# An adaLN block on one core: whole-tile attention, tighter KV products, LayerNorm arithmetic on GpSimd, and DMA transposes of the attention output

## The chip, the cores and the metric

The kernel runs on one core of a Trainium2 chip. The metric is device time in microseconds of one execution, the lower the better. The time of the kernel before is the median of three runs. One execution of each kernel is also recorded by the hardware profiler; all rows in this document come from such records.

## The reference, cut to what matters

One transformer block with adaptive layer norm, on 2048 tokens of 512 features (bf16), 32 heads of 16 features, and a feed-forward width of 1376.

```python
mod = silu(c) @ w_mod                      # six vectors of 512: sa, ca, ga, sb, cb, gb
h = layernorm(x) * (1 + ca) + sa
q, k, v = split_heads(h @ wqkv)            # 32 heads of 16
pq, pk = q @ w_phi, k @ w_phi              # per head
phi_q = concat(softmax(pq), softmax(-pq))  # feature map, 32 values per head
phi_k = concat(softmax(pk), softmax(-pk))
kv, z = phi_k.T @ v, sum_over_tokens(phi_k)
o = (phi_q @ kv) / (phi_q @ z + 1e-6)      # linear attention: no token-by-token matrix
x = x + ga * (o @ wo)
h = layernorm(x) * (1 + cb) + sb
x = x + gb * ((silu(h @ w_gate) * (h @ w_up)) @ w_down)
```

## The kernel before

Tokens are cut into 16 tiles of 128 and 4 chunks of 512. The program does not issue its work in source order. Every piece of work is registered with `pl.op` (line 89) with the engines that may do it, a booked duration `us`, and the buffers that it reads and writes. `Plan.run` (149) then lays all of them out on a time line of its own, with due times from `set_due` (114: each step back along a chain costs STRETCH times the booked duration plus WAIT; the matmuls marked `spine` are SPINE apart; second-norm transposes are PACE apart), and with PSUM and SBUF slots (`slots`, 227) and shares of the PSUM banks by kind (`quota`, 230). What comes out is a fixed order for each engine. On the chip an engine that meets an instruction whose input is not there waits, and all that stands behind it waits too.

Stage one runs over the 16 tiles. `first_norm` (487) makes LayerNorm statistics: `bn_stats` and `bn_aggr` on VectorE (`stats`, 340), then variance plus epsilon on VectorE, power -0.5 on GpSimd and minus mean times that on VectorE (`rstd_of`, 347), then the normalised tile `xn` on VectorE or ScalarE (`normalize`, 368). `first_T` (503) turns it feature-major on TensorE and modulates it (`modulate_T`, 380). `k_tile` (521) makes k through the folded weight `Wk2`, two exponentials on ScalarE (538, 539), their sums `S` and reciprocals `R` on VectorE (548, 549), the product `phik` on GpSimd (551), and v. `kv_tile` (554) adds phik times v into PSUM with 8 matmuls of 129 columns. `q_front` (570) makes q by chunk, and its exponentials `eT`. `gate` (588) makes ga and gb as rows; lines 625 to 631 then scale the weights `wo_sb` (4 instructions) and `wd_sb` (11) by them on GpSimd, in the middle of stage one.

After the last `kv_tile`, lines 635 to 649 write the masked sums into `KVZ`. Then `prepare(k)` (828) does two tiles at a time. `attend` (665) works on half a tile: 4 matmuls of 144 columns into the one buffer `two_ps` (2 PSUM banks), copies `Ssw`, four small VectorE instructions (690 to 695), and two that write `o2` (707). The next half can start only when `two_ps` is free again. `turn` (716) makes `oT`, feature-major: for tiles 0 and 1 by eight matmuls against the identity (726); for tiles 2 to 15 a GpSimd addition `o` (736), four TensorE transposes into a PSUM bank (735) and a ScalarE copy (739). `project` (741) multiplies by `wo`, adds to x and does the second LayerNorm; `second_T` (757) transposes and modulates again.

The feed-forward part runs over six units of two or four tiles (UNITS, 32): `ffn_gu` (773) makes gate and up by blocks of 128 of the 1376 features, `ffn_down` (807) the down projection, the sum with x (824) and the store from SP's queue (826). PSUM has 8 banks: 2 are `two_ps`, 6 are handed out one by one, of which one is an accumulator until the turn from stage one.

## Time and profile before

| | us |
|---|---|
| median of 3 runs (lowest to highest) | 248.45 (248.22 to 249.34) |
| the profiled execution: its own time | 248.46 |
| its span, first to last instruction | 246.7 |
| TensorE matmul busy in the span | 215.0 (87%) |
| VectorE busy | 174.6 (71%) |
| ScalarE busy | 128.3 (52%) |
| GpSimd busy | 101.1 (41%) |

The profiled execution is 0.01 us from the median, and 1.76 us of it lie outside the span. Busy shares over the whole span mix stages with different limits, so the table alone says only that TensorE is the busiest; the rows by stage say which engine is full where.

### The profile page before, as it was taken

To read this page: it belongs to the slowest core of one execution; us is meant where nothing else is said; L and a number is where in the kernel's file an instruction comes from. 1 tells how busy PE (TensorE), PEld (TensorE's weight loads), DVE (VectorE), ACT (ScalarE), POOL (GpSimd) and SP (SyncE) were. 2 spreads that over 40 slices of the span, in tenths; PEclk is the share of its full clock that TensorE was granted. 3 is DMA by queue.
4 is the path that set the end of the run, shared out by engine and by line. 5 is a ranking of instruction groups with operands and counts; after the bars stand their busy time and mean duration, and the time that the engine had idled before them with its cause. 6 is when DMAs were issued, how large, how long until landed. Compare 5 with 4: busy or idle time off the path is not lost.

```text
span 246.7 us, 4221 instructions
## 1 busy us (share of the span) xinstructions
PE 215.0 (87%) x1533; PEld 131.7 (53%) x1556; DVE 174.6 (71%) x461; ACT 128.3 (52%) x280; POOL 101.1 (41%) x100
## 2 busy tenths in 40 slices
PE   0799897939985879999999996999699999699994
PEld 0754555426543437777867853884345454344441
DVE  3779999996957886677767798888744798522122
ACT  2579987564763655943534524563355442355500
POOL 1117788997794011441431443353225242013300
PEclk9999999976997999999999999999999999999999
DMA  7999930000000000001001000001000001100011
GB/s 227 383 406 387 381 103 0 3 0 0 0 4 0 0 1 3 0 0 45 1 3 43 0 4 0 0 24 43 24 0 1 1 0 45 43 0 3 0 41 44
DMA packets 9062, 13.95 MB, mean 57 GB/s; under 512 B 1009, under 2 KB 6482, under 8 KB 9042
## 3 DMA queue, kind: packets, MB, share of 16 engines
q1 hardware_dynamic: 8512, 13.67, 15.4%
q8 instruction: 12, 0.20, 0.3%
q10 hardware_dynamic: 530, 0.02, 0.1%
q14 instruction: 8, 0.07, 0.1%
HBM read 11.58 MB, written 2.10 MB: 55 GB/s over the span
## 4 chain that ended last, share of the span: by engine, by line
PE 64%; DVE 24%; ACT 3%; DMA 3%; issue 3%; POOL 1%; SPq 0%; DVEq 0%; ACTq 0%
PE one_ps L786 31%; PE one_ps L818 14%; DVE S L548 5%; PE one_ps L748 5%; PE two_ps L675 3%; DVE st L343 3%; DMA wmod_sb<-in_w_mod_dram 3%; DVE xn L372 3%; PE one_ps L528 2%; PE one_ps L575 2%; DVE R L549 2%; PE one_ps L532 2%; DVE o L707 2%; ACT hT L396 2%; DVE ln_nmr L361 1%
## 5 line engine op out<-in xcount | busy, mean ns | idle before, releaser
L786 PE MATMUL one_ps<-hT,wg_sb 128*128 128x256 bf16 (+3 forms) x264 | 46.2, 308 | 1.2 <-ACT hT L396 0.9
L786 PE MATMUL one_ps<-hT,wu_sb 128*128 128x256 bf16 (+3 forms) x260 | 45.2, 307 | 0.2
L793 ACT ACTIVATE sg<-one_ps 128x512 bf16<-128x512 f32 (+2 forms) x46 | 26.3, 577 | 28.3 <-PE one_ps L786 25.2
L802 POOL TENSOR_TENSOR gu<-usb,sg 128x512 bf16<-128x512 bf16 (+1 forms) x22 | 23.5, 1070 | 42.7 <-ACT usb L800 39.9
L818 PE MATMUL one_ps<-wd_sb,gu 128*128 128x512 bf16 (+1 forms) x171 | 40.5, 379 | 0.2
L551 POOL TENSOR_TENSOR phik<-e,R 128x1024 bf16<-128x1024 bf16 x16 | 30.7, 1931 | 13.0 <-ACT hT L396 5.5
L786 PEld LDWEIGHTS <-wg_sb 128*128 128x128 bf16 (+1 forms) x264 | 25.9, 100 | 13.9 <-issue 2.1
L786 PEld LDWEIGHTS <-wu_sb 128*128 128x128 bf16 (+1 forms) x264 | 26.0, 100 | 12.2
L736 POOL TENSOR_TENSOR o<-o 128x512 bf16<-128x512 bf16 x14 | 16.1, 1152 | 38.0 <-DVE o L707 33.6
L796 DVE TENSOR_TENSOR gu<-one_ps,sg 128x512 bf16<-128x512 f32 (+1 forms) x24 | 16.3, 685 | 20.3 <-PE one_ps L786 18.4
L357 POOL TENSOR_TENSOR ln_rstd<-ln_veps,mhalf 128x1 f32<-128x1 f32 (+2 forms) x21 | 13.4, 639 | 38.3 <-DVE ln_veps L353 33.7
L818 PEld LDWEIGHTS <-gu 128*128 128x128 bf16 (+1 forms) x176 | 16.7, 98 | 17.0
L707 DVE TENSOR_TENSOR o<-two_ps,A 128x256 bf16<-128x256 f32 x64 | 24.0, 416 | 0.8
L343 DVE BATCH_NORM_STATS2 st<-x_c 128x6 f32<-128x512 bf16 x32 | 21.7, 679 | 2.7 <-DMA x_c<-in_A_x_dram 2.4
L581 ACT ACTIVATE eT<-one_ps 128x512 bf16<-128x512 f32 x32 | 17.5, 599 | 10.3 <-PE one_ps L575 10.3
L675 PE MATMUL two_ps<-KVZ,eT 128*128 128x144 bf16 x128 | 13.7, 232 | 7.3 <-DVE o L707 6.9
L548 DVE TENSOR_REDUCE S<-e 128x64 f32<-128x1024 bf16 x16 | 19.1, 1191 | 1.3 <-ACT e L539 1.2
L388 PE MATMUL one_ps<-ident_b,xn 128*128 128x128 bf16 x128 | 11.9, 236 | 7.1 <-DVE va L544 3.9
L528 PE MATMUL one_ps<-Wk,hT 128*128 128x512 bf16 x61 | 17.2, 399 | 1.0 <-ACT hT L396 0.6
L532 PE MATMUL one_ps<-wqkv_sb,hT 128*128 128x512 bf16 x62 | 17.1, 391 | 0.3 <-DVE st L343 0.2
L675 PEld LDWEIGHTS <-eT 128*128 128x128 bf16 x128 | 10.0, 100 | 13.6 <-DVE o L707 6.0
L748 PE MATMUL one_ps<-wo_sb,oT 128*128 128x512 bf16 x58 | 15.6, 380 | 1.7 <-ACT oT L739 1.4
(89 smaller groups left out, 324.6 us busy)
## 6 DMA issues: line engine op xcount, KB each, us to landing
x_c<-in_A_x_dram SPq DMA_DIRECT2D x4, 512.0 KB, 9.1
wmod_sb<-in_w_mod_dram SPq DMA_DIRECT2D x1, 2048.0 KB, 13.9
out_dram<-ot SPq DMA_DIRECT2D x16, 128.0 KB, 1.8
wqkv_sb<-in_A_wqkv_dram SPq DMA_DIRECT2D x3, 512.0 KB, 8.6
wg_sb<-in_B_w_gate_dram SPq DMA_DIRECT2D x1, 1376.0 KB, 17.5
...
```

The lines of the kernel that those rows point to most:

```text
L343: nc.vector.bn_stats(st6[:], src)
L528: nc.tensor.matmul(pk()[:], lhsT=hT[c_i][k][:, cols], rhs=Wk2[:, k, :], start=(k == 0), stop=(k == KD - 1))
L532: nc.tensor.matmul(v()[:], lhsT=hT[c_i][k][:, cols], rhs=wqkv_sb[:, k, 2 * D:3 * D], start=(k == 0), stop=(k == KD - 1))
L548: pl.op("DVE", r=[e], w=[Ss], us=1.18, fn=lambda: nc.vector.tensor_reduce(Ss()[:], e()[:], axis=AX.X, op=ALU.add))
L551: pl.op("POOL", r=[e, R], w=[bphik[i]], us=1.9, fn=lambda: nc.gpsimd.tensor_tensor(bphik[i]()[:], e()[:], R()[:].unsqueeze(3).to_broadcast ...
L675: nc.tensor.matmul(nd()[:, jj, sg * NDW:(sg + 1) * NDW], lhsT=eTs[c_i, sg, j][:, ts_], rhs=KVZ[:, sg * KD + j, :], start=True, stop=True)
L707: nc.vector.tensor_tensor(o2()[:, sg, half * HK:(half + 1) * HK, :].rearrange("p j (h d) -> p j h d", d=DH), ndv()[:, :, sg, 0:P].rearrang ...
L748: nc.tensor.matmul(a()[:], lhsT=oT()[:, j, :], rhs=wo_sb[:, j, :], start=(j == 0), stop=(j == KD - 1))
L786: nc.tensor.matmul(ps_()[0:fsz, q * n:(q + 1) * n], lhsT=wt[:, k, m * P:m * P + fsz], rhs=h2[k], start=(k == 0), stop=(k == KD - 1))
L793: pl.op("ACT", r=[g, bsilu], w=[sg], us=0.2 + 0.3 * L / CW, fn=lambda: nc.scalar.activation(sg()[0:fsz, 0:L], g()[0:fsz, 0:L], ACT.Silu))
L802: pl.op("POOL", r=[usb, sg], w=[gu], us=0.1 + 1.05 * L / CW, fn=lambda: nc.gpsimd.tensor_tensor(gu()[0:fsz, 0:L], usb()[0:fsz, 0:L], sg()[ ...
L818: nc.tensor.matmul(fp()[:], lhsT=b()[0:fsz, c0:c0 + P], rhs=wd_sb[0:fsz, m, :], start=(m == 0), stop=(m == FM - 1))
```

## The change

- `first_norm` keeps only `bn_stats` on VectorE. Ten small GpSimd instructions a group combine the six statistics into `rstd` and `nmr`. The second LayerNorm keeps `bn_aggr` on VectorE; its other arithmetic is four GpSimd instructions. `normalize` on VectorE multiplies by rstd and adds nmr.
- phi_k is laid out in 8 groups of 4 heads with both signs in one group of 128 columns. `kv_tile` still has 8 matmuls, of 65 columns instead of 129, into two banks instead of three. `KVZ` is written by four pairs of 64 partitions; all of it is zeroed at the start.
- The scaling of `wo_sb` is registered behind the last phik, that of `wd_sb` behind the first part of KVZ.
- `attend` works on a whole tile: 8 matmuls into four banks (`four_ps`, one buffer), and half as many VectorE instructions of twice the width. Those four banks are the two of the kv sums and two of the single ones, so 4 single banks are left after the turn, where there were 6; before the turn there are 6, where there were 5.
- Tiles 2 to 15 are turned by a DMA transpose from SP's queue, SBUF to SBUF, 128 KB each, booked at 2.6 us on a resource of its own (`XBAR`). The four TensorE transposes, their PSUM bank and the ScalarE copy go. There are 3 `oT` buffers instead of 2.
- Chunk 1 is one feed-forward unit of 4 tiles, not two of 2. Due times, quotas and the choice between two engines (the earliest end, not the earliest start) are new.

```diff
-UNITS = [(0, 0, 2), (0, 2, 2), (1, 0, 2), (1, 2, 2), (2, 0, 4), (3, 0, 4)]
+UNITS = [(0, 0, 2), (0, 2, 2), (1, 0, 4), (2, 0, 4), (3, 0, 4)]
-STRETCH = 1.6
-WAIT = 0.8
-SPINE = 1.2
-PACE = 11.0
+STRETCH = 2.54
+WAIT = 1.43
+SPINE = 1.1
+PACE = 8.1
+QUOTA = {'q': 2, 'turn': 4, 'T': 2, 'T2': 4, 'wo': 4, 'down': 4, 'gu': 3, 'kv': 4, 'fold': 2}
+EARLY = ("kv", "q", "fold", "T")
...
-    quota = {"q": 1, "turn": 1, "T": 2, "wo": 1, "down": 2, "gu": 4, "kv": 4, "fold": 3}
+    quota = QUOTA
...
-        pl.op("DVE", r=bmv, w=[b0], us=0.1, fn=f1)
-        pl.op("POOL", r=[b0], w=[b], us=0.4 + 0.15 * n, fn=f2)
-        pl.op("DVE", r=[b] + list(bmv), w=[bn], us=0.1, fn=f3)
+            nc.gpsimd.tensor_scalar_add(veps[:], mv_t()[:, :, 1], LN_EPS)
+            nc.gpsimd.tensor_tensor(st["rstd"][:], veps[:], mhalf[:, 0:n], op=ALU.pow)
+            nc.gpsimd.tensor_scalar(veps[:], mv_t()[:, :, 0], -1.0, None, op0=ALU.mult)
+            nc.gpsimd.tensor_tensor(st["nmr"][:], veps[:], st["rstd"][:], op=ALU.mult)
+        pl.op("POOL", r=bmv, w=[bn], us=0.8 + 0.15 * n, fn=f)
...
+        def f():
+            v = [tmp[:, i, :] for i in range(5)]
+            tt = nc.gpsimd.tensor_tensor
+            tt(v[0], st6[:, :, 1], st6[:, :, 4], op=ALU.subtract)
+            tt(v[1], st6[:, :, 2], st6[:, :, 5], op=ALU.add)
+            tt(v[2], v[0], v[0], op=ALU.mult)
+            nc.gpsimd.tensor_scalar(v[2], v[2], D / 4.0, D * LN_EPS, op0=ALU.mult, op1=ALU.add)
+            tt(v[3], v[2], v[1], op=ALU.add)
+            nc.gpsimd.tensor_scalar(v[3], v[3], 1.0 / D, None, op0=ALU.mult)
+            tt(rstd[:], v[3], mhalf[:, 0:w], op=ALU.pow)
+            tt(v[4], st6[:, :, 1], st6[:, :, 4], op=ALU.add)
+            tt(v[4], v[4], mhalf[:, 0:w], op=ALU.mult)
+            tt(nmr[:], v[4], rstd[:], op=ALU.mult)
+        pl.op("POOL", r=bst, w=[bn], us=1.6 + 0.15 * w, fn=f)
...
-                nc.tensor.matmul(kv_acc(g // 3)[:, (g % 3) * (P + 1):(g % 3 + 1) * (P + 1)],
-                                 lhsT=bphik[i]()[:, sg, 8 * j:8 * j + 8, :].rearrange("p h f -> p (h f)"),
-                                 rhs=bva[i]()[:, j, :], start=(i == 0 and g % 3 == 0), stop=(i == NT - 1),
+                nc.tensor.matmul(kv_acc(g // 4)[:, (g % 4) * (HG + 1):(g % 4 + 1) * (HG + 1)],
+                                 lhsT=bphik[i]()[:, g].rearrange("p s h f -> p (s h f)"),
+                                 rhs=bva[i]()[:, g, :], start=(i == 0 and g % 4 == 0), stop=(i == NT - 1),
...
+    for k in range(KD):
+        pl.op("POOL", r=[bgab[0], bphik[NT - 1]], w=[bwo[k]], us=1.16, fn=lambda k=k: nc.gpsimd.tensor_tensor(
+            wo_sb[:, k, :], wo_sb[:, k, :], gab[:, 0, :], op=ALU.mult))
...
+    for sg in range(2):
+        for r in range(2):
+            def fz(sg=sg, r=r):
...
+            pl.op("DVE", r=[bkv], w=[bKVZ[2 * sg + r]], us=0.65, fn=fz)
+
+    for m in range(FM):
+        fsz = fm_size(m)
+        pl.op("POOL", r=[bgab[1]] + bKVZ[0:1], w=[bwd[m]], us=1.16, fn=lambda m=m, fsz=fsz: nc.gpsimd.tensor_tensor(
+            wd_sb[0:fsz, m, :], wd_sb[0:fsz, m, :], gab[0:fsz, 1, :], op=ALU.mult))
...
-    def attend(n, half):
+    def attend(n):
...
-            for jj, j in enumerate(js):
+            for j in range(KD):
                 for sg in range(2):
...
-            tp = bank("turn", [P, KD, P], BF16)
-            o = sb("qf", "o", [P, KD, P], BF16)
-
-            def f():
-                for j in range(KD):
-                    nc.tensor.transpose(tp()[:, j, :], o()[:, j, :], ident_b[:])
-            pl.op("POOL", r=[o2, second], w=[o], us=1.15, fn=lambda: nc.gpsimd.tensor_tensor(
-                o()[:], o2()[:, 0], o2()[:, 1], op=ALU.add))
-            pl.op("PE", r=[o], w=[tp], us=0.23, fn=f)
+            o = sb("qf", "o", [P, D], BF16)
+            pl.op("POOL", r=[o2], w=[o], us=1.15, fn=lambda: nc.gpsimd.tensor_tensor(
+                o()[:], o2()[:, 0].rearrange("p j m -> p (j m)"), o2()[:, 1].rearrange("p j m -> p (j m)"), op=ALU.add))
+            pl.op("XBAR", r=[o], w=[oT], us=2.6, fn=lambda: nc.sync.dma_start(oT()[:], o()[:], transpose=True))
+            return
```

## Rows read from the trace of the kernel before

**Rows 1.** Busy by stage: window, length, busy of each engine (instructions), granted clock, DMA.

```profile
17.00:58.40 41.40, 34.24 (x293) 21.37 (x296) 40.50 (x63) 32.43 (x61) 33.37 (x23) 0.93 0.40 145
58.40:72.00 13.60, 12.93 (x91) 7.02 (x92) 8.60 (x11) 8.78 (x16) 12.08 (x8) 0.95 0.00 1
72.00:92.20 20.20, 14.75 (x94) 7.66 (x93) 16.33 (x61) 10.62 (x24) 6.11 (x7) 0.92 0.00 1
92.20:243.30 151.10, 143.51 (x974) 88.72 (x987) 98.17 (x289) 68.46 (x167) 46.89 (x50) 1.00 0.04 14
```

**Rows 2.** VectorE groups from 17 to 58.4, one shape a row: busy, mean ns.

```profile
L372 DVE TENSOR_SCALAR xn<-x_c,ln_mv,ln_rstd 128x512 bf16<-128x512 bf16 x6 | 6.6, 1140 | 0.0
L361 DVE SCALAR_TENSOR_TENSOR ln_nmr<-ln_mv,ln_rstd 128x4 f32<-128x4 f32 x3 | 3.4, 1134 | 0.0
L353 DVE TENSOR_SCALAR ln_veps<-ln_mv 128x4 f32<-128x4 f32 x3 | 1.7, 567 | 0.1
L344 DVE BATCH_NORM_AGGREGATE ln_mv<-st 128x2 f32<-128x6 f32 x9 | 1.6, 182 | 0.3
```

**Rows 3.** Timeline near the end of stage one: start, length, instruction, idle before it.

```profile
50.34 3.56 DVE L372 TENSOR_SCALAR xn<-x_c,ln_mv,ln_rstd 128x512 bf16<-128x512 bf16 x2
54.55 1.86 PE L388 MATMUL one_ps<-ident_b,xn 128*128 128x128 bf16 x16 [3.92 <-DVE va L544]
```

**Rows 4.** Costliest groups of the whole span, GpSimd, one shape a row.

```profile
L551 POOL TENSOR_TENSOR phik<-e,R 128x1024 bf16<-128x1024 bf16 x16 | 30.7, 1931 | 13.0 <-ACT hT L396 5.5 <-DVE R L549 3.9 <-PE one_ps L558 2.4
L630 POOL TENSOR_TENSOR wd_sb<-wd_sb,gab 128x512 bf16<-128x512 bf16 x10 | 11.4, 1168 | 0.0
L357 POOL TENSOR_TENSOR ln_rstd<-ln_veps,mhalf 128x4 f32<-128x4 f32 x3 | 3.0, 1006 | 0.1
L326 POOL CAST KVZ<-bm 128x64 bf16<-128x64 f32 x1 | 0.3, 290 | 0.3 <-DVE bm L316 0.3
```

**Rows 5.** The chain that ended last: start, length, engine and line, instructions.

```profile
9.32 1.02 PE one_ps L434 x32
61.56 0.35 PE two_ps L558 x6
111.58 0.45 PE one_ps L388 x8
189.81 0.86 PE one_ps L786 x4
```

**Rows 6.** Timeline of the turn from stage one to the feed-forward part.

```profile
71.38 5.63 POOL L630 TENSOR_TENSOR wd_sb<-wd_sb,gab 128x512 bf16<-128x512 bf16 x5
73.16 0.41 DVE L642 TENSOR_TENSOR KVZ<-one_ps,bm 128x256 bf16<-128x256 f32 x1
73.29 0.41 PE L675 MATMUL two_ps<-KVZ,eT 128*128 128x144 bf16 x4 [0.31 <-DVE KVZ L645]
75.13 0.81 DVE L695 TENSOR_TENSOR A<-Ssw,rden 128x32 f32<-128x32 f32 x1
76.78 0.64 PE L675 MATMUL two_ps<-KVZ,eT 128*128 128x144 bf16 x4 [2.22 <-DVE o L707]
78.47 0.19 DVE L695 TENSOR_TENSOR A<-Ssw,rden 128x32 f32<-128x32 f32 x1
78.69 0.75 DVE L707 TENSOR_TENSOR o<-two_ps,A 128x256 bf16<-128x256 f32 x2
84.26 0.75 DVE L707 TENSOR_TENSOR o<-two_ps,A 128x256 bf16<-128x256 f32 x2
92.19 1.34 PE L786 MATMUL one_ps<-hT,wg_sb 128*128 128x256 bf16 x8
```

**Rows 7.** TensorE's waits from 92.2 to 243.3: total, times, longest.

```profile
PE two_ps L675 <- DVE o L707: 2.8, 2, 1.7
```

**Rows 8.** DMA issues of the span: count, KB each, median us from issue to landing.

```profile
x_c<-in_A_x_dram SPq DMA_DIRECT2D x4, 512.0 KB, 9.1
out_dram<-ot SPq DMA_DIRECT2D x16, 128.0 KB, 1.8
```

More of the change, by code (lines that the diff above doesn't have):

```diff
@@ L133, in room @@
         for i in range(self.slots[b.tag]):
+            if b.tag == "one" and not (b.kind == f"last{i - 4}" if str(b.kind)[:4] == "last" else i < 4 or b.kind in EARLY):
+                continue
             old = live[b.tag].get(i)
@@ L225 @@
     ps = ctx.enter_context(tc.tile_pool(name="ps", bufs=1, space=PSUM))
-    slots = {"one": 6, "two": 1, "xn": 8, "nmr": 4, "ln2": 6, "WT": 2, "e": 3, "S": 3, "R": 3, "phik": 4,
-             "va": 4, "Ssw": 2, "A": 2, "o2": 3, "o": 2, "oT": 2, "sg": 3, "gu": 13,
+    slots = {"one": 6, "four": 1, "xn": 8, "nmr": 4, "ln2": 6, "WT": 2, "e": 3, "S": 3, "SS": 3, "Q": 3, "R": 3, "phik": 4,
+             "va": 4, "Ssw": 2, "A": 2, "o2": 3, "o": 2, "oT": 3, "sg": 3, "gu": 13,
              "usb": 2, "ot": 3}
-    quota = {"q": 1, "turn": 1, "T": 2, "wo": 1, "down": 2, "gu": 4, "kv": 4, "fold": 3}
+    quota = QUOTA
     pl = Plan(slots, quota)
@@ L241, in sb @@
         return Buf(tag, make)
-    two_ps = ps.tile([P, 2, CW], FP32, name="two_ps")
-    one_ps = [ps.tile([P, CW], FP32, name=f"one_ps{i}") for i in range(slots["one"])]
+    early_cm = tc.tile_pool(name="early", bufs=1, space=PSUM)
+    early = early_cm.__enter__()
+    kv_ps = early.tile([P, 2, CW], FP32, name="kv_ps")
+    one_ps = [ps.tile([P, CW], FP32, name=f"one_ps{i}")[:] for i in range(4)]
+    one_ps += [early.tile([P, CW], FP32, name=f"one_ps{i}")[:] for i in range(4, 6)]
+    blast = [Buf("one", kind=f"last{i}", keep=True) for i in range(2)]
+    four_ps = {}
     def bank(kind, shape=(P, CW), dtype=FP32):
         def make(slot):
-            ap = one_ps[slot][:] if dtype == FP32 else one_ps[slot][:].bitcast(dtype)
+            ap = one_ps[slot] if dtype == FP32 else one_ps[slot].bitcast(dtype)
             n = 1
@@ L256, in bank @@
         return Buf("one", make, kind=kind)
-    def pair():
-        return Buf("two", lambda slot: two_ps)
     pools["lnp"] = lnp
@@ L656, in f_turn @@
         modp_cm.__exit__(None, None, None)
+        early_cm.__exit__(None, None, None)
+        four_ps[0] = ctx.enter_context(tc.tile_pool(name="late", bufs=1, space=PSUM)).tile([P, KD, CW], FP32, name="four_ps")
         pools["qf"] = ctx.enter_context(tc.tile_pool(name="qf", bufs=1))
-    pl.op("NONE", r=bKVZ + bgab + [bmodB, bmodA] + bWq2, w=[bturn], us=0.0, fn=f_turn)
+    pl.op("NONE", r=bKVZ + bgab + [bmodB, bmodA] + bWq2, w=[bturn] + blast, us=0.0, fn=f_turn)
     bh2 = [[Buf() for _ in range(KD)] for _ in range(NT // 2)]
@@ L716, in turn @@
+        pl.op("DVE", r=[nd, A], w=[o2], us=1.25, fn=fo)
     def turn(n, on_pe):
-        o2, second = bo2.pop(n)
+        o2 = bo2.pop(n)
         oT = boT[n] = sb("qf", "oT", [P, KD, P], BF16)
@@ L828, in prepare @@
     def prepare(k):
-        a, b = 2 * k, 2 * k + 1
-        attend(a, 0)
-        attend(a, 1)
-        attend(b, 0)
-        turn(a, k == 0)
-        attend(b, 1)
-        project(a)
-        turn(b, k == 0)
-        project(b)
+        for n in (2 * k, 2 * k + 1):
+            attend(n)
+        for n in (2 * k, 2 * k + 1):
+            turn(n, k == 0)
+            project(n)
         h2_guard(k)
```

185 lines of the change are left out of this document (91 added, 94 removed).

## The prediction, made before the changed kernel was run

> **What bounds the kernel now.** I read the busy times by stage first, then VectorE's and GpSimd's groups inside stage one, then the chain of waits and the timeline of the turn, last TensorE's own waits in the feed-forward part. The stages have different limits [rows 1]. From 17.0 to 58.4 VectorE is busy 40.5 of 41.4 us: it is the limit, with TensorE at 34.2. From 58.4 to 72.0 TensorE is (12.9 of 13.6): the last four tiles of k, v and kv. From 72.0 to 92.2 no engine is full (TensorE 14.8, VectorE 16.3 of 20.2): this is latency, the chain attend, turn, project, norm, transpose of tiles 0 and 1, before the first gate matmul at 92.19 [rows 6]. From 92.2 to 243.3 TensorE is busy 143.5 of 151.1, the limit again; 7.6 us are idle, where a unit begins and the preparation of its tiles is late; the largest named wait is for VectorE's o, 2.8 us [rows 7]. Then 3.4 us of last addition and store, which the change doesn't touch.
>
> The sum is made against the profiled execution: span 246.7 us, 1.76 us around it, together 248.46, next to the median of 248.45.
>
> **Part by part.**
>
> *First LayerNorm, VectorE to GpSimd.* Off VectorE between 17 and 58.4 go three nmr (3.4 us), three variance-plus-epsilon (1.7) and nine aggregations (1.6) [rows 2]. An aggregation partly overlaps its neighbours, so I count 0.1 each: 3.4 + 1.7 + 0.9 = 6.0 us. VectorE idles 0.9 us there, so nearly all of it is on the path: -6.0. The nmr instructions are long (1.13 us on 4 elements) because they stand against GpSimd work, and the xn that follow may inherit that wait; so the gain could be as small as 3.
>
> GpSimd gets three groups of ten instructions in that stretch. The power takes 1.0 us; the other nine are bounded above by the 0.29 us of a 64-element cast, so at most 3.6 us a group, 2.6 us more than now [rows 4]. That is paid for by what leaves: 10 + 4 + 1 weight scalings of about 1.17 us, 17.5 us in all, of which 5 (5.6 us) now run after 71.4 [rows 4, 6]. From 17 on GpSimd then has 16 x 1.93 + 3 x 3.6 = 41.7 us at most and could end at 58.7, where the last phik now ends at 71.4, when wd's scalings follow [rows 6]. So it hides the new work, but caps the gain of stage one near 12 us.
>
> *xn.* Six xn on VectorE take 6.6 us, two of them together 3.56 us, and TensorE idles 3.9 us behind that pair before the last first-norm transposes [rows 2, 3]. The change books VectorE's xn at 0.95 and ScalarE's at 0.72 and takes the earlier end, so some of them move. Nothing to all of 3.9 could come back; with ScalarE at 32.4 of 41.4 I take -1.5.
>
> *kv.* Six kv matmuls of 129 columns take 0.35 us, 58 ns each. Half the columns would be 29 ns, but a matmul of one column with its own weights takes 1.02/32 = 32 ns, so 32 is the floor [rows 5]. That saves 8 x 26 = 0.21 us a tile. Only the tail after 58.4 is TensorE's, 5 kv tiles: -1.0. The new phik layout keeps sizes, so exp, S, R and phik cost what they did.
>
> *KVZ.* Now three pairs of instructions, and the first attend (73.29) starts before the last pair is done, 1.25 us after 72.04. In the change four pairs have to be done before any attend. One pair is about 0.41 us for 256 elements [rows 6] plus two small ones, 0.7 us: 2.9 against 1.25, so +1.6.
>
> *attend by tile.* A half that nothing disturbs runs from 76.78 to 79.44, 2.66 us: 1.91 for matmuls, copies and small instructions, 0.75 for o [rows 6]. A whole one adds four matmuls of about 60 ns (144 columns, beside the 58 ns above), 0.24, and up to 0.2 for the wider small instructions, which are mostly fixed cost: 2.35. Its o takes 0.75 to 1.5, say 1.4. That is 3.75 against 5.3 a tile. For tiles 0 and 1 the four halves ran from 73.29 to 85.01, 11.7 us, with 1.0 us of disturbance in the first; two whole ones make 7.5: -4.2. But wo (4) and wd (11) are now scaled on GpSimd just then. The row that shows the price is A at 75.13, 0.81 us beside a wd instruction, against 0.19 alone at 78.47 [rows 6]. Two such instructions a tile, each between 0 and 1.17 us of wait: 0 to 4.7, take 2.3. Sum -1.9. The second norm's power, now with three instructions more, can stand behind a scaling (0 to 1.2): +0.6. Behind tile 2's and 3's scalings wait their o additions, which nothing needs before the second unit.
>
> *Turn by DMA.* Off TensorE go 14 x 4 transposes. A 128-column transpose in a stream takes 0.45/8 = 56 ns [rows 5], so 14 x 0.22 = 3.1 us, where TensorE is the limit: -3.1. The ScalarE copies that go are off the path. In their place stands a DMA that no row shows. The nearest is the 128 KB store, 1.8 us from issue to landing; the far end is a 512 KB load in a crowded queue, 9.1 [rows 8]. Same bytes, an equally empty queue: I take 2 to 3 us, about the 2.6 booked. Then the fixed order already has other matmuls in the time, and it costs nothing. What waits if it is late: `project` on TensorE, with all gate and up matmuls behind it. The transposes share SP's queue with the 16 stores; one queued behind a store waits for that store's sum on VectorE. I put this into the next term.
>
> A rule speaks against this step: the Trainium skill, "VectorE: DVE Perf Modes", section "The three transpose paths", gives 1309 ns for a 128x128 bf16 transpose by DMA against 390 by TensorE, and its rules take TensorE where PSUM will do. Four such blocks one after the other would be 5.2 us a tile, an estimate from that page, and 252 us in all by the first rival's working; the same page speaks of about 90% of DMA bandwidth, by which it would be near the store. Here the row has a TensorE transpose at 56 ns, so the page's ratio is worse still for the DMA; but TensorE's time is what the kernel lacks.
>
> *Feed-forward.* Of 7.6 us idle the change can take what late preparation causes: VectorE does 1.5 us less a tile there, and due times lie further ahead. I take half, -3.8 (0 to -7.6). Against it stand four single banks where six were. A bank is filled in 0.86 us [rows 5], and an emptying instruction can find one o of 0.7 us ahead of it; with three banks for gate and up a late one stops TensorE. I take +2.0 for that and late transposes (0 to 10). One unit of four in place of two of two leaves the columns as they are: nothing.
>
> Sum: -6.0 - 1.5 - 1.0 + 1.6 - 1.9 + 0.6 - 3.1 - 3.8 + 2.0 = -13.1. Span 246.7 - 13.1 = 233.6, and 1.76 around it: 235.4 us.
>
> **The rivals.** (a) *Transposes land late; slower.* The order books 2.6 us plus a hop of 0.2. If they take e longer, each of the 7 pairs of tiles stops TensorE for e (the two of a pair overlap). The gain of 13.1 is gone at e = 1.9, a landing time of 4.7 us, between the ends 1.8 and 9.1. At their middle, 5.4, it is 235.4 + 7 x 2.6 = 253.6. For it: TensorE runs a fixed order. Against it: the bytes and the queue are those of the 1.8 us store, and only the first tiles of a unit are needed at once. It is also where the page of the Trainium skill named above would put the time.
> (b) *Four banks bind.* If about 30 gate or up groups, those beside a preparation, wait 0.3 us each, that is 9 us, 7 more than booked: 242.4. For it: 98 us of VectorE work lie in 151 us. Against it: a pair of o, 0.75 us, is shorter than one fill of 0.86 [rows 5, 6].
> (c) *GpSimd holds the turn.* 15 scalings, 17.5 us, in a stretch of 20 us: if every small VectorE instruction and both powers meet one, 2.4 + 0.6 more, and if wo is late by two scalings, 2.3 more: 240.7.
> (d) *Stage one gives half*, since xn inherits nmr's waits: 3.0 and 1.5 less there, and with none of the idle time recovered, 3.8 less: 243.7. With half of (b), 3.5, it is 247.2: no change. For it: VectorE's instructions beside GpSimd's are long already [rows 2]. Against it: part of xn can go to ScalarE.
>
> **How the numbers follow.** The forecast 0.50, (b) 0.18, (c) 0.12, (d) 0.10, (a) 0.10. The likeliest gives 235.4. Its fast end: cap of stage one (3.5 more), no disturbance (2.3), all idle time back (3.8), no late bank (2.0), together 11.6 if all came at once; I go 7.4 down, to 228. Upwards the range takes in (c), (b) and the faster half of (d), to 246; left out are (a), half of (d) and the fast extreme. A run can tell about 0.5%, 1.2 us. Faster by more: forecast, (b), (c) and half of (d), less a little for (b) grown larger: 0.83. Within: 0.06. Slower: (a) and a little of (d), 0.11.
>
> **What would show it.** Right: first attend near 66.5 to 68, not 73.3; first gate matmul near 84, not 92.2; no 3.9 us TensorE gap before the last first-norm transposes; A and xn near the turn at 0.5 to 1 us; transposes landing in 2 to 3 us; feed-forward part near 146 us with idle time under 6. Wrong: `project` waiting for a DMA in the waits; gate or up matmuls waiting for VectorE or ScalarE; GpSimd without idle time until the last phik, or the first gate matmul still after 90.

## The result, and the profile after

The changed kernel takes 227.43 us (median of 4, 227.23 to 227.87) where the kernel before, measured beside it, takes 248.33 (246.61 to 249.34): a ratio of 0.917, 95% interval 0.911 to 0.922, a gain of 20.9 us. The forecast was 235.4, a gain of 13.1, with a range from 228 to 246: the direction was right, and the gain was larger than the range allowed, by 0.6 us. The profiled execution took 227.87, of which 226.1 is span and 1.77 lies around it. An execution that took over 1.5% longer than the fastest of its kernel is named below and left out of medians and ratios.

Where the time came from is read from the windows by stage, the view of [rows 1], with edges by the work: 62.7 is where the last sums of kv are there (72.0 before), 83.7 the first gate matmul (92.2 before), and 50.7 stands 12 us ahead of the last sums (58.4 before, 13.6 us ahead) (window, length, busy of TensorE matmul, weight load, VectorE, ScalarE, GpSimd with instructions, granted clock, DMA share, GB/s):

```profile
17.00:50.70 33.70, 29.04 (x243) 15.79 (x241) 30.90 (x43) 29.77 (x55) 27.15 (x40) 0.95 0.49 178
50.70:62.70 12.00, 11.68 (x129) 6.43 (x130) 8.78 (x12) 10.02 (x20) 11.85 (x7) 1.00 0.01 1
62.70:83.70 21.00, 17.79 (x122) 9.31 (x120) 16.66 (x42) 17.14 (x35) 19.19 (x24) 1.00 0.00 1
83.70:222.50 138.80, 136.72 (x827) 75.38 (x824) 82.57 (x181) 57.43 (x118) 55.41 (x91) 1.00 0.12 29
```

To 50.7 no engine is full any more: VectorE 30.9, ScalarE 29.8, TensorE 29.0, GpSimd 27.2 of 33.7, where VectorE had 40.5 of 41.4. From 50.7 TensorE is the limit, as it was from 58.4. The turn is fuller (TensorE 17.8 of 21.0, against 14.8 of 20.2) and about as long. The feed-forward part is 138.8 us against 151.1, with 2.1 us of TensorE idle against 7.6.

The prediction left one column of these rows unread, TensorE's granted clock. It has two levels, 2.4 GHz (1.00) and 1.2 GHz (0.50). Between 17 us and the last matmul the kernel before ran at 1.2 GHz twice, the changed kernel once, from 27.6 to 31.1. First the two of before, then the one of after:

```profile
52.90:59.70 6.80, 4.93 (x36) 4.03 (x37) 5.85 (x10) 2.96 (x6) 4.42 (x4) 0.50 0.00 0
76.80:80.20 3.40, 2.81 (x14) 1.71 (x15) 1.84 (x9) 1.03 (x2) 0.21 (x1) 0.51 0.00 0
```

```profile
27.60:31.10 3.50, 3.50 (x10) 1.24 (x9) 2.70 (x5) 1.61 (x4) 3.41 (x6) 0.51 1.07 363
```

The first fell within the 3.92 us of idle time of [rows 3], the second at the end of the 2.22 us of idle time before 76.78 [rows 6], the third 0.9 us behind 2.09 us of idle time. What the two of before cost is at most half of TensorE's busy time in them, 2.5 and 1.4 us (an estimate), all of it ahead of the first gate matmul. In the feed-forward part the clock reads 1.00 in both kernels, so none of its 12.3 us comes from the clock.

| us | before | after | difference | forecast |
|---|---|---|---|---|
| first attend begins | 73.29 | 65.32 | -8.0 | -6.9 |
| first attend to first gate matmul | 18.90 | 18.37 | -0.5 | -1.3 |
| first gate to last down matmul | 151.1 | 138.8 | -12.3 | -4.9 |

The timeline of the turn, lines that answer to [rows 6] (start, length, instruction, idle before it and its releaser):

```profile
62.76 0.41 DVE L671 TENSOR_TENSOR KVZ<-kv_ps,bm 64x256 bf16<-64x256 f32 x1 [2.50 <-PE kv_ps L591]
65.32 0.66 PE L710 MATMUL four_ps<-KVZ,eT 128*128 128x144 bf16 x8
66.68 4.51 POOL L683 TENSOR_TENSOR wd_sb<-wd_sb,gab 128x512 bf16<-128x512 bf16 x4
66.76 1.13 DVE L728 TENSOR_TENSOR den<-U 128x32 f32<-128x32 f32 x1
68.31 0.73 DVE L731 TENSOR_TENSOR A<-Ssw,rden 128x64 f32<-128x64 f32 x1
69.08 1.29 DVE L739 TENSOR_TENSOR o<-four_ps,A 128x512 bf16<-128x512 f32 x2
```

The first KVZ instruction starts at 62.76, where before it started at 72.04; all four pairs have to be done before the attend, 2.6 us (2.9 booked). The disturbance by GpSimd is there as well: `den` takes 1.13 and A 0.73 beside the wd scalings.

TensorE's groups in the feed-forward part, first after and then before (matmul, count, busy, mean ns, idle time before them and its releaser):

```profile
L812 PE MATMUL one_ps<-hT,wg_sb 128*128 128x512 bf16 (+3 forms) x220 | 45.7, 337 | 0.4 <-DVE hT L415 0.4
L812 PE MATMUL one_ps<-hT,wu_sb 128*128 128x512 bf16 (+3 forms) x220 | 45.4, 337 | 0.0
L710 PE MATMUL four_ps<-KVZ,eT 128*128 128x144 bf16 x99 | 8.3, 226 | 0.2 <-DVE o L739 0.2
```

```profile
L786 PE MATMUL one_ps<-hT,wg_sb 128*128 128x256 bf16 (+3 forms) x264 | 46.2, 308 | 1.2 <-ACT hT L396 0.9
L786 PE MATMUL one_ps<-hT,wu_sb 128*128 128x256 bf16 (+3 forms) x260 | 45.2, 307 | 0.2
L675 PE MATMUL two_ps<-KVZ,eT 128*128 128x144 bf16 x104 | 10.8, 226 | 2.8 <-DVE o L707 2.8
L735 PE MATMUL one_ps<-ident_b,o 128*128 128x128 bf16 x56 | 5.4, 219 | 0.0
L575 PE MATMUL one_ps<-hT,Wq 128*128 128x512 bf16 x12 | 3.2, 378 | 0.1
```

Gate and up cost the same. Gone are the transposes (L735) and the twelve q matmuls (L575), three blocks; all q is now done before the first gate matmul. An attend matmul costs TensorE the same as before. A group's busy time counts the modelled end of its last matmul, while the next one already runs, so it looks dearer in groups of four than in groups of eight; from start to start it is 0.25/4 = 62 ns before and 0.49/8 = 61 ns after:

```profile
82.22 0.41 PE L675 MATMUL two_ps<-KVZ,eT 128*128 128x144 bf16 x4
82.47 0.81 PE L575 MATMUL one_ps<-hT,Wq 128*128 128x512 bf16 x3
```

```profile
70.42 0.66 PE L710 MATMUL four_ps<-KVZ,eT 128*128 128x144 bf16 x8 [1.84 <-DVE o L739]
70.91 0.61 PE L754 MATMUL one_ps<-ident_b,o 128*128 128x128 bf16 x8
```

What changed is how many fall into this part: 104 before, 96 after (3 of the 99 in the line began ahead of it), since four tiles and not three are attended ahead of the first gate matmul. And TensorE's wait for `o` [rows 7] has shrunk from 2.8 us to 0.2. What is left of its waits there (total, times, longest):

```profile
PE one_ps L404 <- ACT xn L392: 1.0, 2, 0.5
PE one_ps L404 <- DVE xn L388: 0.5, 1, 0.5
PE one_ps L812 <- DVE hT L415: 0.4, 1, 0.4
PE four_ps L710 <- DVE o L739: 0.2, 1, 0.2
```

No projection waits for a DMA, and no gate or up matmul waits for a bank. The transposes, in the view of [rows 8] (count, median us from issue to landing), are a little slower than the store of the same bytes:

```profile
out_dram<-ot SPq DMA_DIRECT2D x16, 128.0 KB, 1.8
oT<-o SPq DMA_TRANSPOSE x14, 2.4
```

### The profile page after: what moved, and what is told of

It reads as the page before. It is cut to its first block, busy times and chain, and to the rows that moved or that the text cites. A ratio compares the mean times of both kernels' runs of the same rounds, so it can differ in the third digit from the quotient of the medians.

```text
span 226.1 us, 3880 instructions
## 1 busy us (share of the span) xinstructions
PE 205.0 (91%) x1412; PEld 113.9 (50%) x1412; DVE 149.6 (66%) x307; ACT 123.6 (55%) x241; POOL 120.6 (53%) x194
## 2 busy tenths in 40 slices
DMA packets 16678, 15.77 MB, mean 70 GB/s; under 512 B 8625, under 2 KB 14098, under 8 KB 16658
## 4 chain that ended last, share of the span: by engine, by line
PE 66%; DVE 10%; POOL 10%; ACT 5%; issue 4%; DMA 3%; ACTq 0%; DVEq 0%; POOLq 0%
PE one_ps L812 33%; PE one_ps L847 10%; PE one_ps L772 5%; POOL phik L584 4%; PE four_ps L710 4%; PE one_ps L563 4%; PE one_ps L608 3%; PE one_ps L559 3%; DMA wphi_sb<-in_A_w_phi_dram 3%; POOL ln_rstd L378 2%; ACT e L570 2%; ACT xn L392 2%; PE one_ps L404 1%; DVE o L739 1%; PE kv_ps L591 1%
## 5 line engine op out<-in xcount | busy, mean ns | idle before, releaser
L812 PE MATMUL one_ps<-hT,wg_sb 128*128 128x512 bf16 (+3 forms) x220 | 45.7, 337 | 0.4 <-DVE hT L415 0.4
L812 PE MATMUL one_ps<-hT,wu_sb 128*128 128x512 bf16 (+3 forms) x220 | 45.4, 337 | 0.0
L812 PEld LDWEIGHTS <-wg_sb 128*128 128x128 bf16 (+1 forms) x220 | 21.6, 100 | 16.5 <-DVE hT L415 0.5
L812 PEld LDWEIGHTS <-wu_sb 128*128 128x128 bf16 (+1 forms) x220 | 21.8, 100 | 15.7
L392 ACT ACTIVATE xn<-x_c,ln_nmr,ln_rstd 128x512 bf16<-128x512 bf16 x18 | 14.2, 812 | 20.0 <-POOL ln_nmr L380 18.7
L739 DVE TENSOR_TENSOR o<-four_ps,A 128x512 bf16<-128x512 f32 x32 | 20.6, 685 | 0.6
L570 ACT ACTIVATE e<-one_ps 128x512 bf16<-128x512 f32 x32 | 17.2, 612 | 2.5 <-PE one_ps L559 1.3
L563 PE MATMUL one_ps<-wqkv_sb,hT 128*128 128x512 bf16 x64 | 17.8, 403 | 0.0
L608 PE MATMUL one_ps<-hT,Wq 128*128 128x512 bf16 x64 | 15.4, 379 | 0.0
L853 DVE TENSOR_TENSOR ot<-x_c,one_ps 128x512 bf16<-128x512 bf16 x16 | 10.7, 680 | 6.8 <-PE one_ps L847 6.7
L829 ACT CAST usb<-one_ps 128x512 bf16<-128x512 f32 (+1 forms) x21 | 11.9, 565 | 5.1 <-PE one_ps L812 5.0
```

The source lines that it names most:

```text
L563: nc.tensor.matmul(v()[:], lhsT=hT[c_i][k][:, cols], rhs=wqkv_sb[:, k, 2 * D:3 * D], start=(k == 0), stop=(k == KD - 1))
L570: nc.scalar.activation(e()[:, :, sg].rearrange("p g h f -> p g (h f)"), pk()[:].rearrange("p (g n) -> p g n", g=G), ACT.Exp, scale=(1.0, - ...
L608: nc.tensor.matmul(pq()[:], lhsT=Wq2[:, k, j * P:(j + 1) * P], rhs=hT[c_i][k][:], start=(k == 0), stop=(k == KD - 1))
L739: nc.vector.tensor_tensor(o2()[:, sg].rearrange("p j (h d) -> p j h d", d=DH), ndv()[:, :, sg, 0:P].rearrange("p j (h d) -> p j h d", d=DH ...
L812: nc.tensor.matmul(ps_()[0:fsz, q * n:(q + 1) * n], lhsT=wt[:, k, m * P:m * P + fsz], rhs=h2[k], start=(k == 0), stop=(k == KD - 1))
```

## The experiments

What stood to be told apart: why the feed-forward part gained 12.3 us and not 4.9 (the clock is ruled out above). Theory: the plan's new order, and room for it, took out idle time and moved q forward. Rival: one of the parts (the DMA turn, whole-tile attention, units of four) is worth more by its own work than was booked. In "as after" only the named edit differs from the changed kernel; the plan then lays out a new order by itself. Every kernel was compared with the kernel before on the same chip; "over after" below is the difference of medians to 227.43, and the chips' medians of the kernel before lie between 246.9 and 248.6, so 1 us of it means little.

### The turn by DMA

**e1_turn_pe.** As after, but tiles 2 to 15 are turned on TensorE again.

```diff
-            pl.op("XBAR", r=[o], w=[oT], us=2.6, fn=lambda: nc.sync.dma_start(oT()[:], o()[:], transpose=True))
...
+            pl.op("PE", r=[o], w=[tp], us=0.23, fn=f)
```

> The changed kernel (227.4 us) with one part undone: tiles 2 to 15 are turned by four TensorE transposes, a PSUM bank and a ScalarE copy again. If the DMA transposes give only TensorE's time back, the feed-forward part grows by 14 x 0.22 = 3.1 us: 230.5. If they also gave back idle time, because a turn no longer takes one of four single PSUM banks, it grows by 6 us or more, with TensorE idle above 4 us there: 233 or more.

230.19 us (229.81 to 231.02), ratio 0.928 (0.923 to 0.933): 2.8 over after. The feed-forward part grew by 2.8 us to 141.6. The DMA turn is worth what its 56 transposes cost TensorE (3.1 booked), no more; it isn't the missing 7 us.

**e3_dma_twice.** As after, with each transpose issued twice, in the same order of the plan.

```diff
-            pl.op("XBAR", r=[o], w=[oT], us=2.6, fn=lambda: nc.sync.dma_start(oT()[:], o()[:], transpose=True))
+            def f():
+                nc.sync.dma_start(oT()[:], o()[:], transpose=True)
+                nc.sync.dma_start(oT()[:], o()[:], transpose=True)
+            pl.op("XBAR", r=[o], w=[oT], us=2.6, fn=f)
```

> The changed kernel with each DMA transpose issued twice, the second behind the first, while the order still books 2.6 us: a turn takes about 2.4 us longer than booked. By the first rival of the prediction each pair of tiles then stops TensorE for the excess, 7 x 2.4 = 17 us: 244. If the order has enough work between a turn and its projection, at most 1 us is lost: 227 to 228.5.

234.24 us (232.92 to 235.14), ratio 0.942 (0.935 to 0.949): 6.8 over after. TensorE's waits in its feed-forward part name the DMA, five times:

```profile
PE one_ps L775 <- DMA oT<-o: 6.4, 5, 2.7
PE one_ps L404 <- DVE xn L388: 0.5, 1, 0.5
```

This is the prediction's rival (a) made real by one more transpose, some 2.4 us. Its working was that each of seven pairs stops TensorE for the whole excess, 17 us; 6.8 came, in five waits. So the mechanism exists and its price was set 2.5 times too high: the order leaves slack behind most transposes (in the changed kernel the first are issued from 84.45 and the projection that reads them starts at 94.17).

**e6_before_xbar.** The kernel before, with the DMA turn alone and three `oT` buffers.

```diff
...
-            pl.op("PE", r=[o], w=[tp], us=0.23, fn=f)
...
+            pl.op("XBAR", r=[o], w=[oT], us=2.6, fn=lambda: nc.sync.dma_start(oT()[:], o()[:], transpose=True))
+            return
```

> The kernel before with one part of the change: tiles 2 to 15 turned by DMA transposes, three oT buffers. If the DMA transposes give TensorE's 3.1 us and nothing else, as e1_turn_pe says of the changed kernel (2.8 us), 245 to 246. If landing in 2.4 us where a turn on TensorE took 1.2 to 1.9 lengthens the late preparations of this kernel, the gain is lost at the starts of units: 247 to 250.

249.1 us, ratio 1.0056 (1.0016 to 1.0096): no gain at all from the same 3.1 us less on TensorE. The one profiled execution took 444 us, with its matmuls at nearly twice their duration (below), so no trace shows this order at its usual speed. What is on record is the granted clock of the other nine executions, 0.964 to 0.972, where the nineteen of the kernel before beside them read 0.972 to 0.986. At the same 0.971 to 0.972, three of e6 took 247.9 to 249.0 and two of the kernel before 249.3 and 249.6. So some 1 us is there at an equal clock, and the lower clock takes it back. That waits of a late preparation brought the clock down fits this, but isn't shown.

**x1_second_dma.** As after, with the second norm's transposes of tiles 2 to 15 by DMA too.

```diff
+            o_ = pl.op("XBAR", r=[xq], w=[parts[q]], us=2.6, fn=lambda q=q, xq=xq: nc.sync.dma_start(
+                xT()[:, :, q * P:(q + 1) * P], xq()[:], transpose=True))
```

> A step further on the changed kernel: from tile 2 on the second norm's output is also turned by DMA transposes, into SBUF, and modulated from there; no TensorE transposes and no PSUM bank for them. TensorE loses 56 transposes of 56 ns in the feed-forward part, 3.1 us, and four single banks have one user less: 223 to 225. If 2.4 us of transpose come to stand in the path at the starts of units (TensorE waits for hT there), 228 or more.

241.32 us, ratio 0.972 (0.965 to 0.978): 13.9 over after, though TensorE has less to do. Its feed-forward part is 152.0 us with 13.3 idle, at a granted clock of 0.96 on the mean; the first waits in it:

```profile
PE four_ps L710 <- DVE o L739: 7.2, 2, 4.4
PE one_ps L831 <- DVE hT L802: 5.2, 4, 4.2
```

The transposes land in 2.4 us here too. Work taken from the busiest engine is not a gain if the chain that feeds it grows by a landing and a modulation.

### The order

**e2_old_due.** As after, with the four due numbers of the kernel before.

```diff
-STRETCH = 2.54
-WAIT = 1.43
-SPINE = 1.1
-PACE = 8.1
+STRETCH = 1.6
+WAIT = 0.8
+SPINE = 1.2
+PACE = 11.0
```

> The changed kernel with the four numbers of the due times as before (STRETCH 1.6, WAIT 0.8, SPINE 1.2, PACE 11). If the idle time of the feed-forward part (7.6 us before, 2.1 after) went because preparations are due earlier, 3 to 5 us of it return: 230 to 233, with waits of gate matmuls or of the second transposes at the starts of units. If it went because VectorE has less to do, little changes: within 1 us of 227.4.

231.06 us (the middle of three, 230.41 to 232.21; a fourth took 240.57), ratio 0.932 (0.925 to 0.938): 3.6 over after. The first attend moved 3.1 us, to 68.40; the feed-forward part is 1.9 us longer, with the same 2.1 us idle, at a granted clock of 0.99 where after has 1.00. The expected waits where units start did not come: most of what the numbers do lies in stage one here.

**e7_before_due.** The opposite: the kernel before with the new four numbers.

> The kernel before (248.3 us) with nothing changed but the four numbers of the due times (STRETCH 2.54, WAIT 1.43, SPINE 1.1, PACE 8.1). If earlier due times by themselves take idle time away, the 7.6 us idle of the feed-forward part shrink and stage one ends earlier, as e2_old_due lost 4.2 us by the old numbers: 243 to 245. If the numbers only suit the lighter VectorE, it stays at 248 or gets slower.

241.95 us (240.85 to 243.26), ratio 0.980 (0.972 to 0.988): 4.9 less than the 246.86 beside it, with the same work. First attend 69.11 (-4.2), feed-forward part 147.2 with 4.9 idle.

**r1_before_refit.** The kernel before with due numbers chosen for itself: many sets were drawn, and the one for which the plan ends earliest was taken.

```diff
-SLACK = 0.15
-STRETCH = 1.6
-WAIT = 0.8
-SPINE = 1.2
-PACE = 11.0
+SLACK = 0.2
+STRETCH = 1.96
+WAIT = 1.98
+SPINE = 1.18
+PACE = 8.3
```

> The kernel before, all work the same, with STRETCH 1.96, WAIT 1.98, SPINE 1.18, PACE 8.3 and SLACK 0.2, chosen among many for the order that these bookings make shortest. If the order is worth a large part of the 21 us, 236 to 241, with TensorE's named waits from the first gate matmul on below 3 us. If the order matters little without the other parts, not below 242 (e7_before_due, with the change's own numbers: 242.0).

239.6 us (239.28 to 239.74), ratio 0.967 (0.961 to 0.974): 7.5 less than the 247.1 beside it. Its feed-forward part (the columns of [rows 1]) has 3.0 us idle, not 7.6, and eight q matmuls, not twelve:

```profile
88.76:234.09 145.33, 142.30 (x983) 87.71 (x980) 98.67 (x280) 71.19 (x170) 46.62 (x50) 1.00 0.04 15
```

So some 7.5 us were to be had from the old work in a better order. Part of them is the clock: the four executions read 0.991 to 0.993, those of the kernel before beside them 0.972 to 0.986. The first attend is at 68.16, 5.1 us earlier than in the kernel before, the first gate matmul at 88.76, 3.4 earlier. From this kernel to the changed one it is 239.6 - 227.4 = 12.2 us; in the profiled executions 5.1 of them lie ahead of the first gate matmul and 6.5 in the feed-forward part.

**r5_after_refit and r8_rebooked.** Other due numbers for the changed kernel: r5 takes STRETCH 3.14, WAIT 0.52, SPINE 1.02, PACE 11.5; r8 books what the trace of after shows (first-norm chain 2.6 + 0.15 a tile, second 1.15 + 0.15, `xn` on ScalarE 0.81, `o` 1.32) with due numbers chosen for that.

> The changed kernel with STRETCH 3.14, WAIT 0.52, SPINE 1.02, PACE 11.5 in place of its own numbers. Its own order leaves TensorE idle for 2.1 us in the feed-forward part, so there is little to gain: 226 to 228.

> The changed kernel with four bookings taken from its own trace (the first norm's GpSimd chain 2.6 + 0.15 a tile, the second's 1.3, xn on ScalarE 0.81, o 1.32) and STRETCH 3.04, WAIT 0.77, SPINE 1.11, PACE 10.2, SLACK 0.05 chosen for them. If true bookings give an order that TensorE waits less in, 223 to 226. If the order was good enough, 227 to 229.

228.78 (ratio 0.923, 0.917 to 0.930) and 231.66 (0.937, 0.933 to 0.941). Neither beats the changed kernel; true bookings gave a worse order, whose TensorE waits 5.7 us for `o`, 3.5 at once. The plan's end isn't the chip's, even with durations from the chip. None of the kernels run was faster than the changed one.

### What makes room for the feed-forward part

**e4_q_one.** As after, with one PSUM bank for q where two are allowed.

```diff
-QUOTA = {'q': 2, 'turn': 4, 'T': 2, 'T2': 4, 'wo': 4, 'down': 4, 'gu': 3, 'kv': 4, 'fold': 2}
+QUOTA = {'q': 1, 'turn': 4, 'T': 2, 'T2': 4, 'wo': 4, 'down': 4, 'gu': 3, 'kv': 4, 'fold': 2}
```

> The changed kernel with one PSUM bank at a time for q, as before, where it has two. If two banks are what let all q matmuls run before the first gate matmul (three of 16 blocks of 0.86 us ran after it before), three or so fall behind it again and the turn has gaps: 229 to 231. If the q blocks find room because stage one is lighter, no change: 227 to 228.

237.01 us, ratio 0.960 (0.953 to 0.967): 9.6 over after. Twenty q matmuls now stand in the feed-forward part, and TensorE waits beside them (its group there, then its waits):

```profile
L608 PE MATMUL one_ps<-hT,Wq 128*128 128x512 bf16 x20 | 5.3, 378 | 2.5 <-ACT eT L614 2.5
```

```profile
PE one_ps L608 <- ACT eT L614: 2.5, 3, 1.2
PE one_ps L772 <- ACT eT L614: 1.2, 1, 1.2
```

The part is 8.4 us longer (147.2): TensorE is busy 4.0 more in it and idle 4.4 more, of which 3.7 are these waits; the first gate matmul is no earlier for it (84.47). The second q bank, one entry among nine in a dictionary, is what lets TensorE do all q in the turn, where it had time; no order of its own was tried for e4, so what of the 9.6 is misfit isn't known.

**e5_halves, e5b_halves_two.** As after, with attention by halves of a tile again: e5 has one buffer of two banks and leaves the other two idle, e5b two buffers in the four banks.

```diff
-    def attend(n):
+    def attend(n, half):
...
-        nd = Buf("four", lambda slot: four_ps[0])
+        nd = Buf("four", lambda slot: four_ps[0][:, 0:HK, :])
```

and in e5b, which also has two slots for that buffer, not one:

```diff
+        nd = Buf("four", lambda slot: four_ps[0][:, slot * HK:(slot + 1) * HK, :])
```

> The changed kernel with attend by half tiles again, in half of the four-bank buffer. TensorE's four matmuls of a half took 0.33 us of the chain, eight of a whole tile 0.50, so 16 x 0.16 = 2.6 us more TensorE time. VectorE has 1.5 us a tile more to do. If TensorE's own time is what the whole tile saved, 229.5 to 231, with idle time in the feed-forward part below 3 us; if VectorE's relief is what took the idle time away, 232 or more, with 3 us or more of waits for o and xn.

> As e5_halves (260.3 us: attend by half tiles in the changed kernel), but the four banks are two buffers of a half each, so a half need not wait until the one before is read. VectorE's and TensorE's work are those of e5_halves. If what e5_halves lost is the turnaround of its one buffer, most of the 33 us come back: 229 to 235. If it is VectorE's and TensorE's extra work for halves, it stays above 250.

e5: 260.3 us, ratio 1.048 (1.043 to 1.054), 32.9 over after; e5b: 245.45, ratio 0.993 (0.990 to 0.996), 18 over. Waits of the feed-forward part, e5:

```profile
PE four_ps L712 <- DVE o L744: 8.2, 3, 3.0
PE one_ps L404 <- DVE xn L388: 7.2, 3, 3.0
```

The wait for one buffer, the old kernel's own [rows 7], comes back threefold with four banks left for the rest; a second buffer takes half of the loss away. In e5 TensorE is busy 147.1 us there, 10 more than after, at a granted clock of 0.93 on the mean of that part, where after has 1.00; e5b has 142.0 at 0.98. The same matmuls at 1.00 keep it busy for 139.2 us (r3, next), so some 8 of the 10 go with the clock.

**r3_halves_two_refit.** e5b with other due numbers, the four of r5.

> As e5b_halves_two (245.5 us: attend by halves, two buffers), with STRETCH 3.14, WAIT 0.52, SPINE 1.02, PACE 11.5. If halves cost TensorE's 2.1 us and VectorE's 1.5 us a tile, of which VectorE's is hidden under a good order, 229 to 233. If VectorE's extra work is not hidden, it stays at 240 or more.

235.98 us (the middle of three, 235.53 to 238.97; a fourth took 239.83), ratio 0.956 (0.946 to 0.966): 8.6 over after, so some 9 of e5b's 18 were order, clock included. In the profiled execution (235.98) the turn is 4.5 longer (22.9 us from attend to gate against 18.4) and the feed-forward part 5.6 (144.4 against 138.8, VectorE at 96.4 against 82.6), while the first attend is 2.0 earlier. Of the parts undone with another order, whole-tile attention is worth the most. It was booked at -1.9 in the turn and, in the other tiles, only as idle time. The halves here still hold four banks; with two, as in the kernel before, they weren't tried.

**e9_six_units, r4_six_refit.** As after, with chunk 1 as two units of two tiles; r4 with due numbers drawn for that.

```diff
-UNITS = [(0, 0, 2), (0, 2, 2), (1, 0, 4), (2, 0, 4), (3, 0, 4)]
+UNITS = [(0, 0, 2), (0, 2, 2), (1, 0, 2), (1, 2, 2), (2, 0, 4), (3, 0, 4)]
```

> The changed kernel with chunk 1 as two units of two tiles again. The prediction put this part at nothing: 227 to 228.5. If smaller units bring the waits at a unit's start back, or the lighter one-column-block matmuls count, 229 to 231.

> As e9_six_units (233.5 us: chunk 1 as two units of two tiles), with STRETCH 2.1, WAIT 1.47, SPINE 1.1, PACE 11.7 chosen for it. If the part is worth nothing by itself, as the prediction put it, 227 to 229. If the waits at the start of one more unit stay whatever the order, 231 to 234.

233.47 us (ratio 0.940, 0.934 to 0.946) and 229.54 (0.930, 0.924 to 0.935): 6.0 and 2.1 over after. The columns are the same; the 0 that the prediction gave it was about 2 too little in that order. e9's 6.0 holds one long wait of 3.9 us, which r4 lacks (TensorE's waits for VectorE's `xn` after 60 us, e9 and then r4):

```profile
PE one_ps L404 <- DVE xn L388: 4.2, 2, 3.9
```

```profile
PE one_ps L404 <- DVE xn L388: 1.2, 2, 0.9
```

And the wait costs more than itself. In e9 the clock falls within it, and gate and up matmuls behind it run at 1.2 GHz; the same four gate matmuls take 1.91 us at 163.27 and 1.03 at 168.59, when the clock is back (timeline, then the window):

```profile
161.14 0.93 PE L404 MATMUL one_ps<-ident_b,xn 128*128 128x128 bf16 x7 [3.90 <-DVE xn L388]
163.27 1.91 PE L812 MATMUL one_ps<-hT,wg_sb 128*128 128x512 bf16 x4
168.59 1.03 PE L812 MATMUL one_ps<-hT,wg_sb 128*128 128x512 bf16 x4
160.20:167.00 6.80, 5.37 (x23) 2.96 (x25) 4.53 (x12) 1.89 (x5) 2.14 (x4) 0.50 0.10 19
```

In r4 the clock reads 1.00 throughout that part.

### The front parts

**e10_ln_dve, r2_ln_dve_refit.** As after, with the first norm's small operations on VectorE again; r2 with due numbers drawn for that.

```diff
...
+            stats(lambda q=q: mv[:, q, :], x_ch[c_i][:, t, :], [bx[n0 + q]], [bmv[q]])
+        pl.op("DVE", r=bmv, w=[b0], us=0.1, fn=lambda: nc.vector.tensor_scalar_add(veps[:], mv[:, :, 1], LN_EPS))
+        pl.op("POOL", r=[b0], w=[b], us=0.4 + 0.15 * w, fn=lambda: nc.gpsimd.tensor_tensor(
+            rstd[:], veps[:], mhalf[:, 0:w], op=ALU.pow))
+        pl.op("DVE", r=[b] + bmv, w=[bn], us=0.1, fn=lambda: nc.vector.scalar_tensor_tensor(
+            nmr[:], in0=mv[:, :, 0], scalar=-1.0, in1=rstd[:], op0=ALU.mult, op1=ALU.mult))
```

> The changed kernel with the first LayerNorm's small instructions on VectorE as before (aggregation, variance plus epsilon, minus mean times rstd), only the power on GpSimd. By the prediction's first term VectorE's stretch of stage one gets 6.0 us longer, at least 3: the first attend comes 3 to 6 us later than 65.3, and the time is 230.5 to 233.5. If stage one is by now held by GpSimd or ScalarE as much as by VectorE, less than 2 us: 227 to 229.

> As e10_ln_dve (240.1 us: the first norm's small instructions on VectorE again), with STRETCH 2.6, WAIT 0.96, SPINE 1.35, PACE 11.7 chosen for it in the same way. If the work itself costs what the prediction took, 3 to 6 us over the changed kernel: 230.5 to 233.5. If even that was mostly order, 228 to 230. If it is the work, and no order helps, it stays near 240.

240.13 us (ratio 0.967, 0.961 to 0.973) and 231.64 (0.935, 0.927 to 0.942): 12.7 and 4.2 over after. e10 again has one wait of 3.9 for `xn` and ones of 2.1, like the gap of [rows 3], and a granted clock of 0.97 in its feed-forward part:

```profile
PE one_ps L404 <- ACT xn L392: 4.5, 6, 2.1
PE one_ps L404 <- DVE xn L388: 4.4, 2, 3.9
```

In an order of its own the part costs 4.2, within the 3 to 6 that the prediction gave the work, but not where it was booked: the first attend is 2.5 us later (67.85) and the feed-forward part 1.5 longer (140.3).

**e8_scale_early.** As after, with `wo_sb` and `wd_sb` scaled in the middle of stage one.

```diff
-        pl.op("POOL", r=[bgab[0], bphik[NT - 1]], w=[bwo[k]], us=1.16, fn=lambda k=k: nc.gpsimd.tensor_tensor(
+                pl.op("POOL", r=[bgab[0]], w=[bwo[k]], us=1.16, fn=lambda k=k: nc.gpsimd.tensor_tensor(
...
-        pl.op("POOL", r=[bgab[1]] + bKVZ[0:1], w=[bwd[m]], us=1.16, fn=lambda m=m, fsz=fsz: nc.gpsimd.tensor_tensor(
+                pl.op("POOL", r=[bgab[1]], w=[bwd[m]], us=1.16, fn=lambda m=m, fsz=fsz: nc.gpsimd.tensor_tensor(
```

> The changed kernel with the 15 scalings of wo and wd registered in the middle of stage one again. The prediction took 2.9 us of disturbance in the turn for the scalings there; without them the turn (18.4 us from the first attend to the first gate matmul) should be 2 to 3 us shorter. If GpSimd had no room in stage one, the first attend comes later, by as much as 17.5 us of GpSimd work allows: 3 us or more slower in all, 230 to 240. If it had room, 224.5 to 226.

One execution of 236.21 us and three of 242.66 to 243.58, the profiled one among these. It is slower than after by 8.8 us at least. Where, the trace tells of the longer executions only: one wait of 7.9 us for `o` in the turn. What it costs in a fitting order wasn't tried.

## Why the prediction was right and wrong

**Right: what bounds each stage. Right in number, in part by luck: the front part.** Of -8.2 forecast ahead of the first gate matmul -8.5 came. VectorE's full window is gone; the 3.9 us gap [rows 3] is gone; the first attend at 65.32 is a little ahead of the 66.5 to 68 named, the first gate matmul at 83.69 where "near 84" stood. GpSimd took the ten small instructions as told: nine of 0.20 to 0.23 us and a power of 1.03, below the 0.29 bound, and it is now as full as the others (39.0 of 45.7 us from 17 to 62.7). KVZ cost +1.3 for 1.6. Attend by tile and the second norm's power brought -0.5 where -1.3 stood, while TensorE also did 12 q matmuls and one more tile's attend before the first gate matmul.

But that the sum met does not show its terms. The old work in another order has its first gate matmul 3.4 us earlier by itself (r1); the two stretches at 1.2 GHz cost at most 3.9 (the estimate above), the one that is left at most 1.8, and the clock stood in no term (the two overlap: r1 has the first of the stretches no more); and of the 6.0 booked for the first norm in stage one, r2 finds 2.5 there. The "half that nothing disturbs" from 76.78 lies in the second stretch: its matmuls took 0.64 us, where four take 0.41 at 2.4 GHz. And kv's 8 matmuls take 0.26 us, 33 ns each, close to the 32 read as a floor, by chance: the 1.02 us of the 32 one-column matmuls [rows 5] hold the whole of the last one (0.17 us on the mean), so those follow each other (1.02 - 0.17)/31 = 27 ns apart.

**Right: the DMA turn.** Landing in 2.4 to 2.6 us, as bounded by the store; nothing waits for it; -2.8 for 3.1. The rule weighed against it, in the Trainium skill, "VectorE: DVE Perf Modes", section "The three transpose paths", would have given 5.2 us a tile as an estimate. The trace differs: four 128x128 blocks land in 2.4, so that figure for one block doesn't add up by blocks. The preference for TensorE that the Trainium skill states on the same page does not hold for the changed kernel, where TensorE is the limit (2.8 us by e1); in the kernel before the exchange brought nothing (e6).

**Wrong: the feed-forward term.** -4.9 was booked (-3.1 transposes, -3.8 idle, +2.0 late banks and transposes), and -12.3 came. By the windows this is -6.8 of busy time and -5.5 of idle, at a clock of 1.00 before and after. The step that failed is the sizing of the idle time, and that work which moves out of the part stood in no term.
- *Idle.* "I take half" of 7.6, with +2.0 against it, is -1.8 net; 5.5 came back, and no bank and no transpose was late. The bounds were there (0 to 7.6); the half was a choice without a row behind it. r1 shows that 4.6 of the 7.6 go with the order alone, on the old work.
- *q.* Not counted at all: three blocks of 0.86 us, 2.6, left the part for the turn. Of the new quotas the prediction weighed only the three banks for gate and up. e4 shows that another, q's second bank, holds 8.4 us of this part in its place, half of it waits.
- *Attend.* One tile more is attended ahead of the first gate matmul, 8 matmuls of 62 ns, 0.5 us. By itself a whole tile saves TensorE nothing here; what it relieves is VectorE (96.4 us of work in this part in r3, 82.6 after), and TensorE's idle time with it (5.2 and 2.1).

With transposes (-3.1) the busy terms make -6.2 against -6.8 measured; the 0.6 over is not assigned, and some matmul records are missing in the trace of the kernel before.

**The common cause.** The prediction priced work, part by part, and the order only as half of the idle time. Order alone, with the clock that follows it, is worth 7.5 us on the old kernel (r1), 4.9 with the change's own numbers (e7). It is no term to be added to the others, though: undone singly, the first norm costs 12.7 and 4.2 in an order of its own, units 6.0 and 2.1, halves 18 and 8.6. The surplus is seen as one or two long waits (3.9 for `xn`, 3 to 4 for `o`) and as the lower clock that goes with them (e5, e9, e10). So the parts don't add up, and a full split of the 20.9 us isn't to be had from these runs. The share of the new choice between two engines, and of the other quotas, was not tried.

**The rivals.** (a) and (b) did not happen, and the +2.0 for them was too much; e3 prices (a) at 6.8, not 17. (c): the disturbance came, at what the forecast itself held (`den` and A of tiles 0 and 1 took 3.16 us, where four such alone take 0.84: 2.3). (d): stage one gave its whole sum, not half, though by r2 only 2.5 of the first norm's 6.0. The range's fast end was made of idle time, banks, stage one and disturbance; q's 2.6 stood in none of it. Without them 227.4 would have been 230.0, inside the range.
